# Attention and squared-ReLU MLP on one core: six small moves in a hand-scheduled order

## The chip, the cores and the metric

The kernel runs on one core of one Trainium2 chip. The metric is the time of one execution on the device, in microseconds (us), taken as the median of three runs. A core has a matrix engine (TensorE, PE in the profile), a vector engine (VectorE, DVE), an activation engine (ScalarE, ACT), a general engine (GpSimd, POOL) and a queue engine that issues DMA transfers (SyncE, SP). Each engine runs its own list of instructions in order, and waits for the others through semaphores.

## The reference

A transformer block for one sequence of 2048 positions and width 512, all in float32. `x` is normalized, projected to q, k and v, and each of 32 heads attends to eight positions, two apart, going back from its own; then comes `wo` and the residual. The result `h` is normalized again and goes through an MLP with 1792 hidden columns, whose activation is the square of the positive part.

```python
qkv = layernorm(x) @ wqkv                       # 2048x512 @ 512x1536, 32 heads of 16
idx = pos[:, None] - arange(8) * 2              # eight positions, masked where negative
attn = softmax(where(mask, q . k[idx] / 4, -1e9))
h = x + (attn . v[idx]) @ wo                    # 512x512
r = maximum(layernorm(h) @ w1 + b1, 0)          # 512x1792
out = h + (r * r) @ w2 + b2                     # 1792x512
```

## The kernel before, in words

Positions are handled in 16 tiles of 128. Every matrix product is made of three products: each operand is split into a high part in a short format (`xh`, `big_h`, `rh`, `th`; a cast on ACT, function `hi`) and a low part, the rest (`xl`, `big_l`, `rl`, `tl`; a subtraction on DVE or POOL, function `lo`). `mm3` issues the twelve matmuls of one such product: four slices of the contraction, three times.

The program has these stages. At the start, tile by tile, `x` is loaded, its statistics are taken (`x_stats`), it is normalized (`x_norm`), transposed on PE into a bank of accumulators (`x_T`) and split (`hi_T` casts on ACT, `lo_T` subtracts on DVE); q, k and v are made for the first four tiles in 16 slots (`n` in the code), and stored to memory in the order that attention needs. `first_phase(t0)` does q, k and v for the other tiles, two at a time, in slots of two halves (`m` counts halves). Attention is not done on PE: DVE multiplies q with k (`pr<-qp,k`) and the exponentials with v (`pr<-ex,v`), reduces (`ex<-pr`), and POOL adds up the products with v (`pr<-pr`, `o<-pr`). It runs beside the products all the time.

The second phase has passes `u` = 0, 1, 2 over four tiles of the hidden layer at a time: slot `p` does the product with one 128-column block of `w1` for the four tiles (`mm`, then `r`, `rh`, `rl`) and the product with `w2` of the block three slots earlier (`acc`). Between them the next four tiles are prepared: the attention output is transposed and split (`o_T`: `oh`, `ol`), multiplied with `wo` (`wo_product`), added to `x` (`h_add`, which takes the statistics too), normalized (`h_norm`), then b2 is added to it for the later residual (`add_b2`, on POOL), and it is stored (`spill`) until it is needed again (`unspill`). `h_T` transposes the normalized `h` and splits it into `big_l`. In the first pass `w2` is split too (`split_w2`: `w2_h`, and `w2_l` as a part of `big_l` or of `w_x`). The last stage handles the last four tiles in pairs of blocks with fewer products, from sums and differences of slices of `w1` (`t_load`, `t_sums`: `traw`; `t_split`: `th`, `tl`) and of `h` (`s`).

The order is set in the code by a small planner. Each slot has two lists of chores: `at(d, f)` puts `f` into the list run at the end of the slot `d` slots on, and `after(d, f)` into a second list, which is run after the attention of that slot was issued. Between the two, `pump` issues attention steps as long as the planned time of DVE (`now["dve"]`) is behind that of PE (`now["pe"]`). `dve(t)` adds `t` to DVE's planned time; a step of attention more or less in a slot follows from that. `HOLD` is 1.0. The tables `LH`, `OP`, `WP`, `HP`, `HL` give the slots in which `h` is loaded, `o_T`, `wo_product` and `h_T` come. `first_phase` has four banks for `mm` results, the second phase two (`Turn`).

Of the kernel before, what the change touches and what calls it, by code (L numbers as in the profile page):

```python
# [17 lines left out]
FB = F // P  # L18
# [12 lines left out]
SLOW = 1.01, 1.12, 1.08  # L31
DELAY = 3
WJ = 2
XT = 9, 11
OT = 4, 5, 10, 12
WO = 7, 9, 13, 15
HT = 20, 20, 21, 23
# [3 lines left out]
WP = 8, 9, 13, 14  # L41
# [5 lines left out]
HOLD = 1.0  # L47
# [5 lines left out]
def block_kernel(ctx, tc, x, wqkv, wo, w1, b1, w2, b2, out):  # L53
# [42 lines left out]
    def row(name, shape=(P, D), dt=F32):  # L96
        return work.tile(list(shape), dt, name=name, tag="row", bufs=ROWS)
# [4 lines left out]
    due = {}  # L102
    late = {}
    now = {"slot": 0, "pe": 0.0, "dve": 0.0, "sub": -1}

    def at(delta, fn, *a):
        due.setdefault(now["slot"] + delta, []).append((fn, a))

    def after(delta, fn, *a):
        late.setdefault(now["slot"] + delta, []).append((fn, a))  # L110
# [8 lines left out]
    def run(chores):  # L119
        todo = chores.get(now["slot"], [])  # L120
        while todo:
            fn, a = todo.pop(0)
            fn(*a)

    def dve(t):
        now["dve"] += t
# [10 lines left out]
    turn = {"mm": Turn("mm0", "mm1"), "tr": Turn("tr0", "tr1")}  # L137
# [58 lines left out]
    def transposes(src, banks="tr"):  # L196
        tr = turn[banks].tile("tr").rearrange("p (k c) -> p k c", k=KB)
        for k in range(KB):
            nc.tensor.transpose(tr[:, k, :], src[:, k * P:(k + 1) * P], ident)  # L199
        now["pe"] += 0.44  # L200
        return tr
# [14 lines left out]
    def mm3(ps, lh, ll, rh, rl, mid=None, at_=2 * KB):  # L216


        terms = [(lh, rh, k) for k in range(KB)] + [(ll, rh, k) for k in range(KB)]
        terms += [(lh, rl, k) for k in range(KB)]  # L220
        for n, (l, r, k) in enumerate(terms):
            if mid and n == at_:
                mid()
            nc.tensor.matmul(ps, l(k), r(k), start=(n == 0), stop=(n == 3 * KB - 1))  # L224
# [218 lines left out]
    def x_T(t):  # L443
        tr = transposes(xt.pop(t))
        xT[t] = row("xh", (P, KB, P), F32R), row("xl", (P, KB, P), F32R)
        at(0, hi_T, tr, [xT[t][0]])
        after(0, lo_T, tr, [xT[t][0]], [xT[t][1]])
# [62 lines left out]
    def qkv(t, gp, mid=None):  # L510

        ps = turn["mm"].tile("mm")
        xh, xl = xT[t]
        mm3(ps[:, :3 * GP], lambda k: xh[:, k, :], lambda k: xl[:, k, :],
            lambda k: pair(wq_h, k, gp), lambda k: pair(wq_l, k, gp), mid)
        at(1, evac, t, gp, None, ps)
# [79 lines left out]
    def wo_product(t, slots):  # L596
        ps = turn["mm"].tile("wo")
        oh, ol = oT.pop(t)
        mm3(ps, lambda k: oh[:, k, :], lambda k: ol[:, k, :],
            lambda k: wo_h[:, k, :], lambda k: wo_l[:, k, :])  # L600
        for n, (fn, a) in zip(slots, ((h_add, (t, ps)), (h_norm, (t,)), (add_b2, (t,)),
                                      (spill, (t,)))):
            (at if fn is h_add else after)(n, fn, *a)

# [3 lines left out]
    def h_T(t):  # L610
        if t // R == R - 1:
            return last_h_T(t)
        tr = transposes(hn.pop(t), "mm")
        i = t % R
        hs_, ls_ = [a[:, :, i] for a in hh], [a[:, :, i] for a in hl]
        due.setdefault(now["slot"], []).insert(0, (hi_T, (tr, hs_)))
        at(0, lo_T, tr, hs_, ls_)


# [266 lines left out]
    for n in range(16):  # L886
        gp, t = divmod(n, 4)
        qkv(t, gp, (lambda: start_T(t + 1)) if n < 3 else None)
        if n < 2:
            x_norm(n + 2)  # L890
        if n == 0:
            x_stats(3)
        if n < 6:
            for k in (0, 1):
                at(0, hi_wqkv, n // 2 + 1, n % 2 * 2 + k)
                after(0, lo_wqkv, n // 2 + 1, n % 2 * 2 + k,
                      nc.gpsimd if k or n < 2 else nc.vector)
        if n == 1:
            load_wqkv(3)
        if n == 13:  # L900
            consts()
        if n in (5, 6, 12, 14):
            at(0, load_x, n - 1 if n < 7 else n // 2)
        if n in (8, 9):
            at(0, x_stats, n - 4)
        if n in (12, 13):
            at(0, x_norm, n - 8)
        if n in (14, 15):
            x_T(n - 10)
        end_slot(2.09)  # L910


# [2 lines left out]
    def first_phase(t0):  # L915
        def chores(m):
            if t0 + 3 < 16:
                if m in (0, 2):
                    at(0, x_stats, t0 + 2 + m // 2)
                if m in (6, 7):  # L920
                    at(0, x_norm, t0 - 4 + m)
                if m in XT:
                    x_T(t0 + 2 + XT.index(m))
            if t0 + 5 < 16 and m in (6, 9):
                at(0, load_x, t0 + 2 + m // 3)
            if jobs and m % 3 == 0:
                at(0, weight_job)
            k = t0 // 2 * 12 - 72 + m
            if k == 19:
                dve(HOLD)  # L930
            for t in range(R):
                if k == OT[t]:
                    at(0, load_h, t)
                    o_T(t)
                if k == WO[t]:
                    wo_product(t, (1, 3, 4, 6))
                    now["pe"] += 2.73
                if k == HT[t]:
                    h_T(t)
            if k in W2:  # L940
                at(0, load_w2, W2.index(k))

        def half(m):
            end_slot(1.37)
            chores(m)

        for n in range(6):
            chores(2 * n)
            qkv_of(t0 + n % 2, n // 2, lambda: half(2 * n + 1))
            end_slot(1.37)  # L950
# [41 lines left out]
    for u in range(R - 1):  # L992
        now["sub"] = u
        first, end = u == 0, False
        fs = list(range(FB)) if first else [*sorted(place), 12, 13]
        fs += [f for f in range(12) if f not in fs and (u < 2 or f not in ENDS)]
        fs += ENDS if u == 2 else []
        need = [] if first else [f for f in fs if f < 12 and f not in place]
        acc = [psum.tile([P, D], F32, name="acc", tag=tag) for tag in ("acc0", "acc1", "tr0", "tr1")]
        js = range(R)  # L1000


        todo, halves = {}, {}
        for i in js:
            t = R * (u + 1) + i
            if not end:
                a = i // 2 if u == 2 else 0
                for p, *what in ((LH[i] - a, at, 0, load_h, t), (OP[i] - a, o_T, t),
                                 (WP[i] - a, wo_product, t, (0, 1, 2, 3))):
                    todo.setdefault(p, []).append(what)  # L1010
                p, h = (HP[i], i % 2) if u < 2 else HL[i]
                (todo, halves)[h].setdefault(p, []).append((h_T, t))
            todo.setdefault(UP[i], []).append((at, 0, unspill, R * u + i))
        if u == 2:
            for p, *what in ((12, at, 0, t_load, 0), (13, at, 0, t_load, 1), (13, after, 0, t_sums, 0),
                             (14, after, 0, t_sums, 1), (14, at, 1, t_split, 0),
                             (16, after, 1, t_split, 1)):
                todo.setdefault(p, []).append(what)

        def half(p):  # L1020
            run(due)
            for fn, *a in halves[p]:
                fn(*a)

        for p in range(FB + LAG):
            more = 0.0
            if p == FB:
                run(due)
                dve(HOLD)
            for fn, *a in sorted(todo.get(p, []), key=lambda x: x[0] is wo_product):  # L1030
                fn(*a)
                more += 2.73 if fn is wo_product else 0.0
            if p < FB:
                mlp1(u, fs[p])
                more += 2.73
                if first:
                    at(0, split_w2, p)
                    if p + 1 < FB:
                        load_w2(p + 1)
            q = p - LAG  # L1040
            if q >= 0:
                f = fs[q]
                mlp2(u, f, acc, js, q == 0, q == FB - 1,
                     (lambda: half(p)) if p in halves else None)
                more += 2.74
                if f < 12 and (need or first and p < FB - LAG):
                    free.append(place.pop(f))
                    if need:
                        at(1, fetch, need.pop(0))
            end_slot(more)  # L1050
        for i in js:
            at(u // 2, finish, R * u + i, acc[i])
# [3 lines left out]
    u = R - 1  # L1056
# [79 lines left out]
```

## Time and profile before

| what | value |
|---|---|
| median of 3 runs | 518.0 us (517.56 to 518.82) |
| the profiled execution, time | 518.24 us |
| its span, first to last instruction | 516.4 us |
| granted TensorE clock | 1.000 |
| PE busy | 509.3 us |
| DVE, POOL, ACT busy | 377.1, 348.9, 256.7 us |
| PE busy from 20 to 140 us | 119.43 of 120 us |
| PE busy from 214 to 260 us | 45.19 of 46 us |
| PE busy from 424 to 444 us | 19.80 of 20 us |
| memory traffic | 97.37 MB, mean 189 GB/s |

A row of the timeline gives the start and duration of an instruction in us, its engine, its line in the kernel, its operation, the tiles as output and inputs, their shapes, and how many like instructions follow each other; in brackets the idle time of the engine ahead of it and what released it. Busy times of PE are modelled at their ends, so its idle time is read better from the distance between starts.

### The profile page before, as it was taken

To read this page: it belongs to the slowest core of one execution; us is meant where nothing else is said; L and a number is where in the kernel's file an instruction comes from. 1 tells how busy PE (TensorE), PEld (TensorE's weight loads), DVE (VectorE), ACT (ScalarE), POOL (GpSimd) and SP (SyncE) were. 2 spreads that over 40 slices of the span, in tenths; PEclk is the share of its full clock that TensorE was granted. 3 is DMA by queue.
4 is the path that set the end of the run, shared out by engine and by line. 5 is a ranking of instruction groups with operands and counts; after the bars stand their busy time and mean duration, and the time that the engine had idled before them with its cause. 6 is when DMAs were issued, how large, how long until landed. Compare 5 with 4: busy or idle time off the path is not lost.

```text
span 516.4 us, 7610 instructions
## 1 busy us (share of the span) xinstructions
PE 509.3 (99%) x2508; PEld 430.4 (83%) x2508; DVE 377.1 (73%) x524; ACT 256.7 (50%) x498; POOL 348.9 (68%) x430
## 2 busy tenths in 40 slices
PE   8999999999999999999999999999999999999997
PEld 7998788888887888877888888888888888999996
DVE  5469899989997798978789799878883025842333
ACT  4624586767424753453364334246433425765542
POOL 4714789894785895796768759767799445585520
PEclk9999999999999999999999999999999999999999
DMA  8677889989767895666477627657541352444112
GB/s 267 182 211 202 247 292 314 285 262 285 236 190 191 276 313 176 176 190 210 137 252 227 174 91 223 202 169 249 177 135 39 102 161 81 159 131 141 64 41 82
DMA packets 88239, 97.37 MB, mean 189 GB/s; under 512 B 8328, under 2 KB 56712, under 8 KB 88200
## 3 DMA queue, kind: packets, MB, share of 16 engines
q1 hardware_dynamic: 87256, 96.37, 60.4%
q10 hardware_dynamic: 944, 0.52, 0.3%
q8 instruction: 19, 0.31, 0.2%
q14 instruction: 20, 0.16, 0.1%
HBM read 72.65 MB, written 24.25 MB: 188 GB/s over the span
## 4 chain that ended last, share of the span: by engine, by line
PE 51%; DVE 3%; DMA 2%; issue 1%; ACT 1%; POOL 1%; DVEq 0%; ACTq 0%
PE acc L805 23%; PE mm L224 15%; PE mm L728 6%; PE wo L224 5%; DMA k<-qkv_d 2%; PE tr L199 1%; DVE pr L335 1%; POOL big_l L144 0%; DVE big_l L144 0%; PE half L828 0%; POOL h L587 0%; ACT big_l L141 0%; DVE ex L369 0%; ACT wo_h L141 0%; DVE pr L346 0%
## 5 line engine op out<-in xcount | busy, mean ns | idle before, releaser
L403 POOL TENSOR_TENSOR pr<-pr 128x512 f32<-128x512 f32 (+1 forms) x128 | 131.9, 1031 | 52.2 <-DVE pr L346 47.0
L224 PE MATMUL mm<-big_l,w_h 128*128 128x512 f32 x336 | 89.6, 393 | 0.8 <-DVE ol L144 0.5
L335 DVE TENSOR_TENSOR pr<-qp,k 128x1024 f32<-128x1024 f32 x64 | 77.0, 1202 | 8.3 <-ACT qp L264 7.1
L346 DVE TENSOR_TENSOR pr<-ex,v 128x1024 f32<-128x1024 f32 x64 | 78.0, 1221 | 5.5 <-POOL o L403 2.9
L369 DVE TENSOR_REDUCE ex<-pr 128x64 f32<-128x1024 f32 x64 | 78.5, 1226 | 1.9
L224 PEld LDWEIGHTS mm<-big_l,w_h 128*128 128x128 f32 x336 | 62.3, 188 | 14.4 <-DVE ol L144 0.9
L144 POOL TENSOR_TENSOR rl<-r,rh 128x512 fp32r<-128x512 f32 x42 | 55.1, 1314 | 24.1 <-ACT rh L141 24.0
L781 ACT ACTIVATE r<-mm,b_sb 128x512 f32<-128x512 f32 x42 | 28.8, 686 | 58.4 <-PE mm L224 52.3
L224 PE MATMUL mm<-big_h,xl 128*128 128x512 f32 (+1 forms) x208 | 56.4, 380 | 0.6 <-DVE xl L144 0.3
L224 PE MATMUL mm<-big_h,xh 128*128 128x512 f32 (+1 forms) x208 | 53.3, 378 | 0.7 <-ACT xh L141 0.7
L805 PE MATMUL acc<-big_l,rh 128*128 128x512 f32 x190 | 52.7, 391 | 0.0
L224 PE MATMUL mm<-big_l,xh 128*128 128x512 f32 (+1 forms) x208 | 52.7, 375 | 0.0
L805 PE MATMUL acc<-big_h,rh 128*128 128x512 f32 x190 | 52.3, 392 | 0.0
L805 PE MATMUL acc<-big_h,rl 128*128 128x512 f32 x190 | 51.8, 390 | 0.0
L493 ACT COPY y<-mm 128x512 f32<-128x512 f32 (+1 forms) x52 | 28.6, 554 | 39.1 <-PE mm L224 26.3
L224 PE MATMUL mm<-big_l,w_l 128*128 128x512 f32 x168 | 45.0, 390 | 0.0
L224 PEld LDWEIGHTS mm<-big_h,xh 128*128 128x128 f32 x208 | 37.7, 188 | 7.2 <-ACT xh L141 1.8
L224 PEld LDWEIGHTS mm<-big_l,xh 128*128 128x128 f32 x208 | 38.2, 188 | 5.9
L224 PEld LDWEIGHTS mm<-big_h,xl 128*128 128x128 f32 x208 | 37.0, 188 | 6.7 <-DVE xl L144 1.9
L805 PEld LDWEIGHTS acc<-big_h,rl 128*128 128x128 f32 x190 | 35.7, 188 | 7.5
L805 PEld LDWEIGHTS acc<-big_l,rh 128*128 128x128 f32 x190 | 35.4, 188 | 7.2
L805 PEld LDWEIGHTS acc<-big_h,rh 128*128 128x128 f32 x190 | 34.8, 188 | 6.6
(148 smaller groups left out, 882.2 us busy)
## 6 DMA issues: line engine op xcount, KB each, us to landing
k<-qkv_d SPq DMA_DIRECT2D x48, 288.0 KB, 2.7
v<-qkv_d SPq DMA_DIRECT2D x48, 288.0 KB, 3.9
qkv_d<-y SPq DMA_DIRECT2D x18, 512.0 KB, 3.4
big_l<-w2l_d SPq DMA_DIRECT2D x24, 256.0 KB, 3.1
xt<-in_A_x_dram SPq DMA_DIRECT2D x16, 256.0 KB, 4.9
q<-qkv_d SPq DMA_DIRECT2D x32, 128.0 KB, 3.5
h<-in_A_x_dram SPq DMA_DIRECT2D x16, 256.0 KB, 3.5
h_d<-h SPq DMA_DIRECT2D x16, 256.0 KB, 3.7
```

What stands on the lines that cost most here:

```text
L144: eng.tensor_tensor(out=dst, in0=src, in1=h, op=ALU.subtract)
L199: nc.tensor.transpose(tr[:, k, :], src[:, k * P:(k + 1) * P], ident)
L224: nc.tensor.matmul(ps, l(k), r(k), start=(n == 0), stop=(n == 3 * KB - 1))
L335: nc.vector.tensor_tensor(out=pr.rearrange("p i w h d -> p i w (h d)"), in0=qps["now"][:, j % 2].unsqueeze(2).to_broadcast([P, RI, W, GC]) ...
L346: nc.vector.tensor_tensor(out=p2, in1=vwin, op=ALU.mult, in0=e1[:, :, :, j * GH:(j + 1) * GH].unsqueeze(4).to_broadcast([P, RI, W, GH, DH]))
L369: nc.vector.tensor_reduce(out=lf[:, :, :, j * GH:(j + 1) * GH], in_=pr, axis=X, op=ALU.add)
L403: nc.gpsimd.tensor_tensor(out=dst, in0=p2[:, :, :w], in1=p2[:, :, w:2 * w], op=ALU.add)
L493: nc.scalar.copy(y[:, :, t % RI * GC:(t % RI + 1) * GC], ps[:, :j * GC].rearrange("p (j c) -> p j c", j=j))
L728: nc.tensor.matmul(ps, sta[y][:, k], mov[x][:, k], start=(first and q == 0), stop=(last and q == len(terms) - 1), skip_group_check=True)
L781: nc.scalar.activation(r, ps, AF.Relu, bias=b1_sb[:, f:f + 1])
L805: nc.tensor.matmul(acc[j], l[:, j * P:(j + 1) * P], w[f], start=(first and n < len(js)), stop=(last and n >= len(terms) - len(js)))
```

## The change

Six places are touched.

1. `x_norm` and `x_T` of tiles 4 and 5 come one slot earlier at the start (`n` 11, 12 and 13, 14 instead of 12, 13 and 14, 15).
2. In `first_phase(12)`, `x_norm` of tiles 14 and 15 comes one half earlier, and their `x_T` at `m` = 7, 8 instead of 9, 11.
3. `h_T` puts the casts ahead of the other chores of the slot only if `mm` has two banks; with four banks they come in their turn.
4. `add_b2` goes into the first list of the next slot instead of the second list of its own. In pass 2, for the last two of the four tiles, `add_b2` and `spill` come three slots later still.
5. In passes 0 and 1 the planner's time of DVE is moved on by `HOLD` once more, at slot `p` = 12 (`FB - 2`).
6. In pass 2, the loads of the second pair, the sums and the splits of both pairs come a slot or two earlier.

```diff
-XT = 9, 11
+XT = (9, 11), (7, 8)
...
-            (at if fn is h_add else after)(n, fn, *a)
+            (after if fn in (h_norm, spill) else at)(n + (fn is add_b2), fn, *a)
...
-        due.setdefault(now["slot"], []).insert(0, (hi_T, (tr, hs_)))
+        if len(turn["mm"].tags) > 2:
+            at(0, hi_T, tr, hs_)
+        else:
+            due.setdefault(now["slot"], []).insert(0, (hi_T, (tr, hs_)))
         at(0, lo_T, tr, hs_, ls_)
...
-        if n in (12, 13):
-            at(0, x_norm, n - 8)
-        if n in (14, 15):
-            x_T(n - 10)
+        if n in (11, 12):
+            at(0, x_norm, n - 7)
+        if n in (13, 14):
+            x_T(n - 9)
...
-                if m in (6, 7):
-                    at(0, x_norm, t0 - 4 + m)
-                if m in XT:
-                    x_T(t0 + 2 + XT.index(m))
+
+                early = t0 == 12
+                if m + early in (6, 7):
+                    at(0, x_norm, t0 - 4 + m + early)
+                if m in XT[early]:
+                    x_T(t0 + 2 + XT[early].index(m))
...
-                                 (WP[i] - a, wo_product, t, (0, 1, 2, 3))):
+                                 (WP[i] - a, wo_product, t, (0, 1, 2 + 3 * a, 3 + 3 * a))):
...
-            for p, *what in ((12, at, 0, t_load, 0), (13, at, 0, t_load, 1), (13, after, 0, t_sums, 0),
-                             (14, after, 0, t_sums, 1), (14, at, 1, t_split, 0),
-                             (16, after, 1, t_split, 1)):
+            for p, *what in ((12, at, 0, t_load, 0), (12, at, 0, t_load, 1), (13, after, 0, t_sums, 0),
+                             (13, after, 0, t_sums, 1), (13, at, 1, t_split, 0),
+                             (14, after, 0, t_split, 1)):
...
+            if u < 2 and p == FB - 2:
                 dve(HOLD)
```

The rows that follow are the programs' instructions in issue order: line, operation, output and inputs, shape. First GpSimd in pass 0, around the low part of a block of `w2` (`big_l<-raw_2467`); `h<-h,b_sb` is `add_b2`, `o<-pr` the end of an attention sum. Before:

```order
L403 TENSOR_TENSOR o<-pr 128x2x64
L587 TENSOR_TENSOR h<-h,b_sb 128x512
L144 TENSOR_TENSOR big_l<-raw_2467,big_h 128x512
L144 TENSOR_TENSOR rl<-r,rh 128x512
L587 TENSOR_TENSOR h<-h,b_sb 128x512
L144 TENSOR_TENSOR rl<-r,rh 128x512
```

After:

```order
L403 TENSOR_TENSOR o<-pr 128x2x64
L144 TENSOR_TENSOR big_l<-raw_2467,big_h 128x512
L587 TENSOR_TENSOR h<-h,b_sb 128x512
L144 TENSOR_TENSOR rl<-r,rh 128x512
L587 TENSOR_TENSOR h<-h,b_sb 128x512
L144 TENSOR_TENSOR rl<-r,rh 128x512
```

The low part of `w2` now stands ahead of the addition of b2.

Next VectorE some ten microseconds later in the same pass: `w_x` is the low part of a block of `w2`, `ol` that of the attention output, `h<-wo,h` and the two rows behind it are `h_add`. Before:

```order
L346 TENSOR_TENSOR pr<-ex,v 128x1024
L369 TENSOR_REDUCE ex<-pr 128x16x4
L144 TENSOR_TENSOR w_x<-raw_2595,w_x 128x512
L144 TENSOR_TENSOR ol<-tr,oh 128x512
L577 TENSOR_TENSOR h<-wo,h 128x512
L152 BN_STATS st<-h 128x6
L153 BN_AGGR mv<-st 128x2
L335 TENSOR_TENSOR pr<-qp,k 128x1024
```

After:

```order
L346 TENSOR_TENSOR pr<-ex,v 128x1024
L144 TENSOR_TENSOR w_x<-raw_2594,w_x 128x512
L144 TENSOR_TENSOR ol<-tr,oh 128x512
L577 TENSOR_TENSOR h<-wo,h 128x512
L152 BN_STATS st<-h 128x6
L153 BN_AGGR mv<-st 128x2
L369 TENSOR_REDUCE ex<-pr 128x16x4
L335 TENSOR_TENSOR pr<-qp,k 128x1024
```

The reduction of attention moved behind `h_add`.

Last VectorE at the end of pass 2, from the last `h_add` to the split of `h` for the last stage; `traw` are the sums of the second pair, `big_l` and `s` parts of `h`. Before:

```order
L577 TENSOR_TENSOR h<-wo,h 128x512
L152 BN_STATS st<-h 128x6
L153 BN_AGGR mv<-st 128x2
L144 TENSOR_TENSOR big_l<-tr,big_l 128x2x128 x4
L696 TENSOR_TENSOR traw<-traw 128x2x128
L697 TENSOR_TENSOR traw<-traw 128x2x128
L698 TENSOR_TENSOR traw<-traw 128x2x128
L699 TENSOR_TENSOR traw<-traw 128x2x128
L663 TENSOR_TENSOR s<-tr,s 128x2x128
L664 TENSOR_TENSOR s<-s,tr 128x2x128
```

After:

```order
L577 TENSOR_TENSOR h<-wo,h 128x512
L152 BN_STATS st<-h 128x6
L153 BN_AGGR mv<-st 128x2
L699 TENSOR_TENSOR traw<-traw 128x2x128
L700 TENSOR_TENSOR traw<-traw 128x2x128
L701 TENSOR_TENSOR traw<-traw 128x2x128
L702 TENSOR_TENSOR traw<-traw 128x2x128
L144 TENSOR_TENSOR big_l<-tr,big_l 128x2x128 x4
L144 TENSOR_TENSOR tl<-traw,th 128x512
L666 TENSOR_TENSOR s<-tr,s 128x2x128
L667 TENSOR_TENSOR s<-s,tr 128x2x128
```

The four sums moved ahead of the splits of `h`, and a part of the second pair's split stands ahead of `s`.

More of the change, by code (lines that the diff above doesn't have):

```diff
@@ L1028, in block_kernel @@
                 run(due)
+                dve(HOLD)
+            if u < 2 and p == FB - 2:
                 dve(HOLD)
```

## The prediction

> **What bounds the kernel now.** I read the engine table first, then TensorE's waits, then the chain that ended last, and then TensorE's timeline row by row, because the table alone shows only that TensorE (PE) is never long idle.
>
> ```profile
> PE 509.3 (99%) x2508; PEld 430.4 (83%) x2508; DVE 377.1 (73%) x524; ACT 256.7 (50%) x498; POOL 348.9 (68%) x430
> ...
> PE mm L224 <- DVE ol L144: 0.5, 1, 0.5
> PE tr L199 <- ACT y L493: 0.4, 1, 0.4
> PE mm L224 <- ACT r L781: 0.3, 1, 0.3
> ...
> 241.27 2.72 PE acc L805 x12
> ```
>
> The reader is to see that the whole span is one stream of matmuls, and that the waits are single events of half a microsecond. The last line is a piece of the chain: 12 matmuls of 512 columns take 2.72 us, 0.227 each, so 4 in a row take 0.91. Wherever the next group starts later than that, PE stood still. Only such stops can be won, since the change leaves the number of matmuls alone. In all rows below the first number is the start, the second the duration, and the bracket the idle time and its releaser.
>
> **The start, x's fifth and sixth parts.** The change puts their normalization and transposes one slot ahead.
>
> ```profile
> 44.82 1.17 PE L224 MATMUL mm<-big_h,xh 128*128 128x512 f32 x4
> 46.31 1.21 PE L224 MATMUL mm<-big_h,xl 128*128 128x512 f32 x4 [0.32 <-DVE xl L144]
> ...
> 48.28 1.08 PE L224 MATMUL mm<-big_h,xh 128*128 128x512 f32 x4
> 49.49 1.19 PE L224 MATMUL mm<-big_h,xl 128*128 128x512 f32 x4
> ...
> 58.28 0.29 DVE L358 TENSOR_REDUCE sm<-ex 128x16 f32<-128x128 f32 x1 [1.56 <-ACT ex L392]
> 63.75 0.68 DVE L144 TENSOR_TENSOR xl<-tr,xh 128x512 fp32r<-128x512 f32 x1
> ...
> 64.49 1.19 PE L224 MATMUL mm<-big_h,xl 128*128 128x512 f32 x4
> ```
>
> The two stops are 1.49 - 0.91 = 0.58 and 1.21 - 0.91 = 0.30, together 0.88. In the new order both xl stand ahead of attention work on VectorE (DVE), so they go. But the seventh part's xl keeps its place, and the matmul at 64.49 starts right when it ends (63.75 + 0.68 = 64.43). That xl is not set by PE: DVE had waited 1.56 at 58.28 for an exponential of ScalarE (ACT) and worked without a pause from there. If PE comes 0.88 sooner, it waits 0.88 longer at 64.49. I count 0; the bounds are 0.88 won (if the exponential comes sooner too) and a loss of the 0.30 that one such stop cost. The move of parts 14 and 15 near 140 us has no PE stop beside it; it stands at 0, between the same bounds of one stop, 0.30 either way.
>
> **The copy ahead of h's parts.**
>
> ```profile
> 157.56 1.20 ACT L141 CAST big_l<-tr 128x256 fp32r<-128x256 f32 x4 [2.30 <-PE tr L199]
> 158.62 0.63 ACT L493 COPY y<-mm 128x512 f32<-128x512 f32 x1
> ...
> 158.28 0.61 PE L224 MATMUL mm<-big_h,xl 128*128 128x512 f32 x2
> 159.30 0.65 PE L199 MATMUL tr<-ident,hn 128*128 128x128 f32 x4 [0.41 <-ACT y L493]
> ```
>
> The third transposes need the bank that y empties, and y stands behind four casts of 1.20 us. PE lost 1.02 - 2 x 0.227 = 0.57. With y ahead of the casts it is done about 1.1 sooner. The casts then end 0.6 later (y's length); the products that read them belong to the next phase, and each lo part on DVE waits for its own cast only. Gain 0.57; bounds 0 and 0.57, the loss excluded since nothing else waits for these casts.
>
> **b2's addition a slot later.**
>
> ```profile
> 225.01 1.29 POOL L587 TENSOR_TENSOR h<-h,b_sb 128x512 f32<-128x512 f32 x1
> 226.26 1.81 POOL L144 TENSOR_TENSOR big_l<-raw,big_h 128x512 fp32r<-128x512 f32 x1
> ...
> 228.11 0.69 ACT L781 ACTIVATE r<-mm,b_sb 128x512 f32<-128x512 f32 x1 [3.67 <-POOL big_l L144]
> ...
> 227.90 0.60 PE L199 MATMUL tr<-ident,o 128*128 128x128 f32 x4
> 228.85 1.19 PE L224 MATMUL mm<-big_l,w_h 128*128 128x512 f32 x4 [0.35 <-ACT r L781]
> ...
> 252.94 0.60 PE L199 MATMUL tr<-ident,hn 128*128 128x128 f32 x4
> 253.29 1.63 PE L805 MATMUL acc<-w_x,rh 128*128 128x512 f32 x6
> ```
>
> PE waits for r, r for big_l, and big_l stood behind the 1.29 of the addition on GpSimd (POOL). Four transposes hold PE 0.35 (252.94 to 253.29), so this stop is 0.95 - 0.35 = 0.60. The new order has big_l first, and r is ready 1.25 sooner: the stop goes. The addition ends where big_l ended, about 228.1; the store of h, queued on SyncE (SP) behind other transfers, was not issued before that anyway.
>
> **Less attention in two slots.** The first two passes of the second phase hold one attention step (1.0 us of the planner's clock) two slots ahead of the end.
>
> ```profile
> 235.72 1.23 DVE L369 TENSOR_REDUCE ex<-pr 128x64 f32<-128x1024 f32 x1
> 236.85 0.75 DVE L144 TENSOR_TENSOR w_x<-raw,w_x 128x512 fp32r<-128x512 f32 x1
> 237.53 0.68 DVE L144 TENSOR_TENSOR ol<-tr,oh 128x512 fp32r<-128x512 f32 x1
> ...
> 236.72 1.07 PE L224 MATMUL wo<-wo_l,ohl 128*128 128x512 f32 x4
> 238.26 1.19 PE L224 MATMUL mm<-big_l,w_h 128*128 128x512 f32 x4 [0.47 <-DVE ol L144]
> ...
> 235.88 0.62 ACT L141 CAST w_x<-raw 128x512 fp32r<-128x512 f32 x1 [0.22 <-DMA raw<-in_B_w_dram]
> ...
> 228.10 0.32 SPq L984 DMA_DIRECT2D w2l_d<-big_l  x1
> ...
> 230.45 0.38 SPq L954 DMA_DIRECT2D raw<-in_B_w_dram  x1
> ```
>
> The stop is 238.26 - 236.72 - 0.91 = 0.63. The reduction (1.23) moves behind ol and h's addition, so w_x can start at 235.72 instead of 236.85, and ol ends at 238.21 - 1.13 = 237.08. Counting the 0.60 of the stop before, PE asks for ol at 237.03. So the two stops together (1.23) bring what ol allows, 1.13 or a little more. This has a condition: w_x's cast waited for its load until 235.88, the load was issued at 230.45, and SP had stood at 228.10 until POOL's big_l was done. Since big_l now ends some 1.25 sooner, the load does too, and the cast at about 234.9 is in time. Were it not, w_x could start only at 236.50 and ol would end at 237.9: the two stops would bring 0.3. I take 1.13, bounds 0.3 and 1.23.
>
> In the other pass the same hold lets DVE write h's last lo parts ahead of a reduction:
>
> ```profile
> 346.52 1.09 PE L805 MATMUL acc<-big_h,rl 128*128 128x512 f32 x4
> 347.63 1.17 PE L224 MATMUL mm<-big_l,w_h 128*128 128x512 f32 x4
> ...
> 250.85 0.76 DVE L144 TENSOR_TENSOR big_l<-tr,big_l 128x256 fp32r<-128x256 f32 x2 [0.56 <-ACT big_l L141]
> ```
>
> That stop is 1.11 - 0.91 = 0.20 and goes (bounds 0 and 0.20). What was held has to be done later: in the first pass a product with v (1.22 by the row of the same length, 1.23 for a reduction) now stands behind the fourth addition to h, and delays the softmax subtraction, ACT's exponential, the norm behind it and the casts. The lo parts of 250.85 would end at 251.61 + 1.22 = 252.83, and the transposes that need their bank start at 252.94. That leaves 0.11. I count 0; if the chain is later still, the loss is what exceeds 0.11.
>
> **The first pairs' weight sums a slot sooner.**
>
> ```profile
> 433.74 1.39 DVE L699 TENSOR_TENSOR traw<-traw 128x256 f32<-128x256 f32 x1
> ...
> 436.25 1.29 POOL L587 TENSOR_TENSOR h<-h,b_sb 128x512 f32<-128x512 f32 x1
> ...
> 436.46 1.35 DVE L144 TENSOR_TENSOR big_l<-s,big_l 128x256 fp32r<-128x256 f32 x1
> 439.08 0.43 DVE L144 TENSOR_TENSOR big_l<-s,big_l 128x256 fp32r<-128x256 f32 x1
> ...
> 438.59 0.40 PE L728 MATMUL mm<-big_l,w_h 128*128 128x256 f32 x2
> 443.02 0.50 PE L728 MATMUL mm<-wo_h,th 128*128 128x256 f32 x2
> ```
>
> From 438.59 to 443.02 PE issues 30 matmuls of 256 columns; at half of 0.227 they need 3.4, and PE took 4.43. Some 0.1 of that is the slower rate of short matmuls, so the three stops are about 0.9. They come from h's last splits on DVE, which stood behind the four sums (the last of 1.39), and one of which took 1.35 beside POOL's addition at 436.25 against 0.43 alone. Now the sums fall into DVE's idle time after the last addition to h, and POOL's addition goes into the last stage. The split chain ends 1.15 + 0.92 sooner: all 0.9 goes (bounds 0 and 0.9). The second pair's four loads move a slot ahead on SP too, and the last two stores of h a slot back, where they hold up a load of w2 by the time that POOL's addition takes; these loads are issued several slots before their use, so I count 0. POOL's two additions (2 x 1.29) now stand around the third pair's sums, and the tl behind them has, by an estimate, half a microsecond of room.
>
> That DVE and POOL can block each other is what 436.46 shows. The Trainium skill (SBUF — State Buffer, "Who interferes with whom") says it more strictly: a VectorE instruction with two SBUF inputs and a GpSimd instruction that reads SBUF exclude each other for the whole instruction. This row agrees; no row of before shows the moved additions in their new place.
>
> **The sum.** 0.57 + 1.13 + 0.20 + 0.9 = 2.8; the first multiplications after each stop are slower as well (46.31 to the next group), which I do not price, and set against the tight places. 2.8 to 3.0, say 2.9. The profiled execution took 518.24, 0.24 above the median of the runs; it would become 515.3, and the median 515.1. I predict 515.2.
>
> **The rivals.**
> - The early stops are kept too. If the exponential at 58 us follows PE, the 0.88 is won: 514.3. Against it speaks DVE's unbroken work from 58.28.
> - A new gate gives 1 to 2 us back. Either w_x's load does not move (0.8 lost: 516.0), or a moved POOL addition meets a two-input DVE instruction that PE waits for, 1.35 - 0.43 = 0.92 each, two of them 1.84: 517.0. For it: it is what 436.46 did. Against it: POOL's additions now stand where DVE has short work. By the page's rule every such meeting costs its length; the rows leave it open.
> - The change does nothing on balance: stops are replaced by the part that was next late, 517.5 to 518.5. For it speaks the narrow room (0.11 and 0.05) at two places; against it that five places are independent.
> - Slower: the held attention is late at the end of its pass. A whole step (product, reduction, product with v: about 3.65) then stands before h's last norms; beyond the 0.11 of room PE waits 3.5 in a pass. That decides if DVE's queue has no idle time left there: 518.8 for one pass, 522.3 for both. Against it: DVE idles 0.56 at 250.85 alone, and only one instruction of 1.2 is held, not a step.
>
> **How the numbers follow.** Forecast (514.4 to 516.2) 0.55; early stops kept 0.10; a new gate (516.2 to 517.3) 0.18; nothing on balance 0.09; slower 0.08. A measurement of this kernel can tell 0.3% (1.55 us) from no change, so faster means under 516.45: the first two and a quarter of the third, 0.69. Slower means over 519.55: 0.05, the second half of the last case. The rest is 0.26. The range from 513.9 to 517.6 leaves out half of the second case, most of the fourth and the last; the forecast's own is 514.4 to 516.2.
>
> **What would show it.** After the change the waits of PE should no longer name ol, y and r; at 64 us the wait for xl should have grown to about 1.2; POOL's big_l should come ahead of h near 225; the three stops after 438 should be gone. Wrong would be a new wait of PE near 250 (casts or lo parts), one for tl in the last stage, or a wait for r or ol that stays.

## The result, and the profile after

The changed kernel takes 515.25 us (median of 9 runs, 514.67 to 517.83) against 517.99 us (9 runs, 517.50 to 518.96): 2.74 us less, a ratio of 0.9950 with a 95% interval of 0.9937 to 0.9962. The profiled execution took 514.81 us, 3.43 less than the profiled one of before; its span is 513.0 us. So the two profiles differ by 0.7 us more than the medians do. That remainder is one of the things to explain.

The engine table, and the waits of TensorE (PE), of the changed kernel:

```profile
PE 506.4 (99%) x2508; PEld 429.3 (84%) x2508; DVE 376.7 (73%) x524; ACT 256.2 (50%) x498; POOL 350.0 (68%) x430
```

```profile
PE tr L856 <- POOL mhalf L842: 1.3, 1, 1.3
PE tr L199 <- DVE xt L190: 1.1, 1, 1.1
PE mm L224 <- ACT xh L141: 0.7, 1, 0.7
PE mm L224 <- DVE xl L144: 0.2, 1, 0.2
```

The busy times hardly move. What went is in the waits: ol, y and r are gone from the list; xl stays once, the rest is the first ten microseconds. Where the time was won is read best from the start of the same matmul in both traces; the difference runs ahead at each stop that went, and falls back at each new one. All starts are from the traces of before and after:

| matmul of before, start | start after | ahead by | what lies in between |
|---|---|---|---|
| 64.49 mm<-big_h,xl | 63.45 | 1.03 | the two stops at 46 and 49 us, with the slower matmuls behind them |
| 160.95 mm<-big_l,xh | 159.38 | 1.57 | the stop for y (0.55) |
| 228.85 mm<-big_l,w_h | 226.70 | 2.14 | the stop for r (0.57, and 0.04 behind it) |
| 249.94 acc<-w_x,rh | 247.11 | 2.84 | the stop for ol (0.66) |
| 299.95 acc<-w_x,rh | 297.35 | 2.60 | a new stop near 252 us (-0.24) |
| 438.59 mm<-big_l,w_h | 435.71 | 2.88 | the stop at 347.63 (0.28) |
| 447.67 acc<-big_h,rh | 443.86 | 3.81 | three stops of the last splits (0.93) |
| 460.00 mm<-wo_l,w_h | 456.58 | 3.42 | a new stop near 450 us (-0.39) |
| 513.05, the last | 509.64 | 3.42 | nothing |

In the table a stop counts with the slower matmuls right behind it, up to 0.1. The rows of PE's timeline after at the places that the prediction speaks of:

```profile
157.78 0.60 PE L199 MATMUL tr<-ident,hn 128*128 128x128 f32 x4
...
226.35 0.60 PE L199 MATMUL tr<-ident,o 128*128 128x128 f32 x4
226.70 1.17 PE L224 MATMUL mm<-big_l,w_h 128*128 128x512 f32 x4
...
234.56 1.08 PE L224 MATMUL wo<-wo_l,ohl 128*128 128x512 f32 x4
235.47 1.13 PE L224 MATMUL mm<-big_l,w_h 128*128 128x512 f32 x4
...
438.58 0.40 PE L731 MATMUL mm<-big_l,w_h 128*128 128x256 f32 x2
438.82 0.40 PE L731 MATMUL mm<-big_l,w_l 128*128 128x256 f32 x2
439.06 0.40 PE L731 MATMUL mm<-big_l,w_h 128*128 128x256 f32 x2
439.31 0.40 PE L731 MATMUL mm<-wo_h,th 128*128 128x256 f32 x2
```

From the transposes at 226.35 to the product it is 0.35, the bare length of four transposes; from 234.56 to 235.47 it is 0.91, four matmuls. Pairs of short matmuls near 439 us follow each other every 0.24 without a gap: all three stops after 438 us are gone. The reasons on VectorE (DVE) and ScalarE (ACT):

```profile
234.06 0.68 DVE L144 TENSOR_TENSOR w_x<-raw,w_x 128x512 fp32r<-128x512 f32 x1
234.66 0.68 DVE L144 TENSOR_TENSOR ol<-tr,oh 128x512 fp32r<-128x512 f32 x1
235.67 0.69 DVE L577 TENSOR_TENSOR h<-wo,h 128x512 f32<-128x512 f32 x1 [0.33 <-PE wo L224]
...
155.78 0.59 ACT L493 COPY y<-mm 128x512 f32<-128x512 f32 x1 [1.43 <-PE mm L224]
156.26 1.21 ACT L141 CAST big_l<-tr 128x256 fp32r<-128x256 f32 x4
...
224.78 0.69 ACT L784 ACTIVATE r<-mm,b_sb 128x512 f32<-128x512 f32 x1 [1.89 <-POOL big_l L144]
```

ol ends at 235.34, 0.13 ahead of the product at 235.47, where before it was 0.6 behind; that product does not read ol, it waits for the bank of accumulators that ol empties. y comes ahead of the casts. r ends at 225.47, 1.2 ahead of PE.

The two new stops, on PE and on what releases it (GpSimd is POOL):

```profile
252.10 0.65 PE L199 MATMUL tr<-ident,hn 128*128 128x128 f32 x4
...
251.23 0.82 ACT L194 ACTIVATE hn<-h,rs 128x512 f32<-128x512 f32 x1 [1.57 <-POOL rs L162]
...
247.19 2.13 POOL L403 TENSOR_TENSOR pr<-pr 128x512 f32<-128x512 f32 x2
249.40 0.47 POOL L403 TENSOR_TENSOR o<-pr 128x128 f32<-128x128 f32 x1
249.95 0.23 POOL L158 TENSOR_SCALAR rs<-mv 128x1 f32<-128x1 f32 x1
...
446.27 1.76 POOL L587 TENSOR_TENSOR h<-h,b_sb 128x512 f32<-128x512 f32 x1
447.98 1.76 POOL L144 TENSOR_TENSOR tl<-traw,th 128x512 fp32r<-128x512 f32 x1
...
449.25 0.40 PE L731 MATMUL mm<-big_l,th 128*128 128x256 f32 x2
449.79 0.50 PE L731 MATMUL mm<-big_l,tl 128*128 128x256 f32 x2
```

Near 252 us the last norm of h waits for three small instructions (rs; the first is shown) on POOL, and these stand behind an attention sum, as they did before. POOL had worked without a pause since 240.76, where another sum had waited 3.50 for DVE's product with v; the hold has put a reduction (1.20) between the addition to h and that product. The norm ends at 252.05, and the transposes start at 252.10. Near 450 us tl ends at 449.74, behind an addition of b2 that took 1.76; PE goes on at 449.79.

### The profile page after: what moved, and what is told of

Same layout as the page of the kernel before. It is cut to its first block, busy times and chain, and to the rows that moved or that the text cites. A ratio compares the mean times of both kernels' runs of the same rounds, so it can differ in the third digit from the quotient of the medians.

```text
span 513.0 us, 7625 instructions
## 1 busy us (share of the span) xinstructions
PE 506.4 (99%) x2508; PEld 429.3 (84%) x2508; DVE 376.7 (73%) x524; ACT 256.2 (50%) x498; POOL 350.0 (68%) x430
## 4 chain that ended last, share of the span: by engine, by line
PE 92%; POOL 3%; DMA 2%; DVE 1%; issue 1%; ACT 1%; SPq 0%; POOLq 0%; ACTq 0%
PE mm L224 45%; PE acc L808 29%; PE wo L224 9%; PE mm L731 6%; PE tr L199 4%; DMA wraw<-in_A_wqkv_dram 1%; DMA qkv_d<-y 1%; POOL pr L403 1%; POOL h L587 1%; POOL tl L144 0%; PE half L831 0%; SPq L432 0%; POOL wo_l L144 0%; DVE pr L346 0%; DVE ex L369 0%
## 5 line engine op out<-in xcount | busy, mean ns | idle before, releaser
L346 DVE TENSOR_TENSOR pr<-ex,v 128x1024 f32<-128x1024 f32 x64 | 78.0, 1221 | 11.6 <-POOL o L403 7.6
L493 ACT COPY y<-mm 128x512 f32<-128x512 f32 (+1 forms) x52 | 28.6, 552 | 40.0 <-PE mm L224 30.1
```

The lines of the kernel that those rows point to most:

```text
L346: nc.vector.tensor_tensor(out=p2, in1=vwin, op=ALU.mult, in0=e1[:, :, :, j * GH:(j + 1) * GH].unsqueeze(4).to_broadcast([P, RI, W, GH, DH]))
L493: nc.scalar.copy(y[:, :, t % RI * GC:(t % RI + 1) * GC], ps[:, :j * GC].rearrange("p (j c) -> p j c", j=j))
```

## The experiments

Each kernel was timed against the kernel before on the same chip. Times below are medians; the stops are from each run's own trace. The changed kernel's 515.25 us, to which differences are taken, comes from its own comparison. The intervals of the ratios reach 0.0012 to 0.0026 either way, 0.6 to 1.3 us, so a difference of medians under about 1 us is not told from nothing by itself; where a smaller one is read below, it is read from the traces.

**The start: two kernels that change only that part.** The first is the kernel before with the first hunk of the change, the second the changed kernel without it.

```diff
-        if n in (12, 13):
-            at(0, x_norm, n - 8)
-        if n in (14, 15):
-            x_T(n - 10)
+        if n in (11, 12):
+            at(0, x_norm, n - 7)
+        if n in (13, 14):
+            x_T(n - 9)
```

> The kernel before with only the start's part of the change (x_norm and x_T of tiles 4 and 5 a slot earlier). Theory 1: the stop near 64 us follows PE, so the 0.9 us of the two early stops is kept: 0.9 faster than before, stop near 64 us still about 0.3 us. Theory 2: the xl of the seventh part is paced by a store of q, k and v that lands near 33 us, and what is won at 46 and 49 us is waited for at 64 us: 0 to 0.3 us faster in the median, and in the trace the end of that xl follows the landing of the store by 30 to 31 us (before 64.43 - 33.88 = 30.55, after 63.40 - 32.25 = 31.15), with a stop near 64 us that is longer where the store lands late.

> The changed kernel without the start's part. Theory 1: two stops near 46 and 49 us are back and it is 0.9 us slower than the changed kernel (about 516.1). Theory 2: the stops are back, but the stop near 64 us shrinks by as much, and it is 0 to 0.3 us slower (about 515.4).

The first took 517.75 against 517.87 of before, a ratio of 0.9998 (0.9985 to 1.0011): no difference that these runs can tell. The second took 515.67 (ratio to before 0.9966, 0.9940 to 0.9992), 0.4 above the changed kernel's median, which these runs can't tell from nothing. What is plain is in its trace. It has the old order, and yet no stop near 46 and 49 us, which neither theory expected. Its stop near 64 us is there in full. What differs between the executions is when transfers land. The row to compare is ACT's copy of y near 33 us, which waits for the store of an older y to land. First before (with two more of its rows, for below), then after, then these two, each with the xl near 64 us:

```profile
32.05 0.69 DVE L152 BATCH_NORM_STATS2 st<-xt 128x6 f32<-128x512 f32 x1 [3.17 <-DMA xt<-in_A_x_dram]
...
33.98 0.86 ACT L493 COPY y<-mm 128x384 f32<-128x384 f32 x2 [5.86 <-DMA qkv_d<-y]
...
56.78 0.59 ACT L493 COPY y<-mm 128x512 f32<-128x512 f32 x1 [0.69 <-DMA qkv_d<-y]
```

```profile
32.35 0.86 ACT L493 COPY y<-mm 128x384 f32<-128x384 f32 x2 [4.36 <-DMA qkv_d<-y]
...
62.72 0.68 DVE L144 TENSOR_TENSOR xl<-tr,xh 128x512 fp32r<-128x512 f32 x1
```

```profile
32.80 0.86 ACT L493 COPY y<-mm 128x384 f32<-128x384 f32 x2 [5.09 <-DMA qkv_d<-y]
...
62.37 0.68 DVE L144 TENSOR_TENSOR xl<-tr,xh 128x512 fp32r<-128x512 f32 x1
63.10 1.19 PE L224 MATMUL mm<-big_h,xl 128*128 128x512 f32 x4 [0.20 <-DVE xl L144]
```

```profile
32.61 0.86 ACT L493 COPY y<-mm 128x384 f32<-128x384 f32 x2 [4.65 <-DMA qkv_d<-y]
...
62.83 0.68 DVE L144 TENSOR_TENSOR xl<-tr,xh 128x512 fp32r<-128x512 f32 x1
63.57 1.20 PE L224 MATMUL mm<-big_h,xl 128*128 128x512 f32 x4 [0.17 <-DVE xl L144]
```

The profile of before came from an execution in which this store landed late, at 33.88. In the others with the loads in the old place it landed between 32.2 and 33.3, and the xl near 64 us ended 29.6 to 31.2 us behind the landing. The landing varies by 1.7 us among executions, and the start's part of the change alone did not move the median: so the first row of the table above is, as far as these runs can tell, luck of the two profiled executions. It is enough for the 0.7 us by which the profiles differ more than the medians. No trace has the new order with a landing as late as that of before.

The early landing is one link of a chain and not the gate itself: between 32.2 and 33.3 it does not order the executions (the xl ends at 62.60 with the landing at 33.02, at 63.33 with 32.21). The copy of y near 55 us is nearer to the gate: in all thirteen traces the xl ends 7.65 or 7.66 us behind its start (before 56.78 and 64.43), and in eleven of them the profile names the landing of a later store as what it waited for, in two a product of PE. The exponential that VectorE (DVE) waits for stands behind this copy on ACT, so by the names in eleven traces it follows transfers and not PE.

**The transfers that pace the start.** If that is so, the stores should be made to land sooner. Two loads of x, 0.5 MB, stand ahead of the early one in the queue of SyncE (SP); here they are issued behind it, and the statistics that need them come a slot later on DVE. Once this is done in the kernel before, alone, and once together with two repairs that are told below.

```diff
-        if n in (5, 6, 12, 14):
-            at(0, load_x, n - 1 if n < 7 else n // 2)
-        if n in (8, 9):
-            at(0, x_stats, n - 4)
+        if n == 7:
+            at(0, load_x, 4)
+            at(0, load_x, 5)
+        if n in (12, 14):
+            at(0, load_x, n // 2)
+        if n in (9, 10):
+            at(0, x_stats, n - 5)
```

> The kernel before, with only the loads of x's tiles 4 and 5 issued behind the first pair of stores that attention waits for. Theory 1: the landing of that store paces the attention of the start, so that all three xl stops of before (near 46, 49 and 64 us) go or shrink: 0.6 to 1.3 us faster than before, about 517. Theory 2: in the kernel before, the stops near 46 and 49 us come from the order on VectorE alone: only the one near 64 us can go, 0 to 0.4 us faster.

> The kernel with both repairs, and at the start the loads of x's tiles 4 and 5 issued behind the first pair of stores of q, k and v that attention waits for, instead of ahead of it. Theory 1: the landing of that store (32.2 to 33.9 us in the runs so far) sets the xl near 64 us; without 0.5 MB ahead of it in the queue it lands 1 to 2 us sooner, the xl comes sooner by as much, and the stop of 0.45 near 64 us goes: 0.4 us faster than with the repairs alone, about 514.2. Theory 2: the xl is set by later transfers, and nothing changes at 64 us; or the statistics of tiles 4 and 5 come late on VectorE and cost up to 1 us near 40 us.

Alone it took 516.68 against 517.52 of before, a ratio of 0.9983 (0.9970 to 0.9995), 0.84 us less. No xl stop is left in its trace, which is of an execution of 518.43, 1.75 above the median, with PE behind by more than a microsecond since the first 12 us. Together with the repairs it took 513.58 (513.55 to 515.24), a ratio of 0.9931 (0.9909 to 0.9952): 1.0 below the repairs alone, more than expected; in the traces the two are 0.89 apart from 64 us on, about half of it the stop there. Its rows:

```profile
31.45 0.48 ACT L493 COPY y<-mm 128x384 f32<-128x384 f32 x1 [3.58 <-PE mm L224]
...
60.88 0.68 DVE L144 TENSOR_TENSOR xl<-tr,xh 128x512 fp32r<-128x512 f32 x1
...
61.99 1.09 PE L224 MATMUL mm<-big_h,xh 128*128 128x512 f32 x4
62.92 1.07 PE L224 MATMUL mm<-big_h,xl 128*128 128x512 f32 x4
```

This copy now waits for PE and no longer for the landing, the xl is 1.4 us ahead of its reader, and the matmuls near 62 us follow without a gap. The start is paced by transfers, then, and the start's part of the change is worth nothing that these runs can tell; that is theory 2 of the first pair, except that the stop near 64 us does not grow with a later landing. By which way the loads' new place helps is not separated: DVE no longer waits for x's load ahead of attention either (3.17 at 32.05 in the trace of before), since the statistics moved too.

**The hold and b2's addition.** First the changed kernel without the hold, then with b2's addition back in its own slot.

```diff
-            if u < 2 and p == FB - 2:
-                dve(HOLD)
```

> The changed kernel without the hold at slot 12 of passes 0 and 1. Theory 1: the stops for r and for ol hang together, since ol's time is set by VectorE and GpSimd and not by PE: a stop of about 1.2 us for ol comes back near 237 us, the stop of 0.27 near 345 us too, and the new stop of 0.23 near 252 us goes: 1.2 us slower than the changed kernel. Theory 2: the two gains add up independently: a stop of 0.63, and 0.67 us slower. Theory 3: ol was late only because the load for w_x came late, which the move of b2's addition cures: no stop for ol, and no difference.

```diff
-            (after if fn in (h_norm, spill) else at)(n + (fn is add_b2), fn, *a)
+            (at if fn is h_add else after)(n, fn, *a)
```

> The changed kernel with all additions of b2 back at the end of their own slot (the last two of pass 2 still three slots late). Theory 1 (the sum as predicted): the stop for r near 226 us comes back with 0.6; ol then has 0.6 more time, but the load of w_x waits behind big_l again, so ol keeps a stop of up to 0.25; the addition ahead of the last stage's first product leaves tl in time and takes the 0.4 away there: 0.2 to 0.5 us slower than the changed kernel. Theory 2: the hold alone sets ol, and POOL's order does not matter: no stop for r, 0.4 faster.

Without the hold: 516.20, a ratio of 0.9972 (0.9958 to 0.9986), 0.95 above the changed kernel. The rows of this kernel:

```profile
233.94 1.23 DVE L369 TENSOR_REDUCE ex<-pr 128x64 f32<-128x1024 f32 x1
235.07 0.74 DVE L144 TENSOR_TENSOR w_x<-raw,w_x 128x512 fp32r<-128x512 f32 x1
235.74 0.68 DVE L144 TENSOR_TENSOR ol<-tr,oh 128x512 fp32r<-128x512 f32 x1
...
234.40 1.08 PE L224 MATMUL wo<-wo_l,ohl 128*128 128x512 f32 x4
236.47 0.74 PE L224 MATMUL mm<-big_l,w_h 128*128 128x512 f32 x2 [1.00 <-DVE ol L144]
```

The stop for ol is 236.47 - 234.40 - 0.91 = 1.16, not the 0.63 of before: what PE won at r it waits for at ol, as theory 1 said. The stop of 0.2 near 345 us is back too, and that near 252 us is gone, with rs 0.5 earlier and PE 1.1 later there.

With the addition back: 515.16 (ratio 0.9945, 0.9927 to 0.9962), no slower than the changed kernel. Its trace, again PE's rows:

```profile
225.86 0.60 PE L199 MATMUL tr<-ident,o 128*128 128x128 f32 x4
226.81 1.21 PE L224 MATMUL mm<-big_l,w_h 128*128 128x512 f32 x4 [0.36 <-ACT r L784]
...
234.72 1.08 PE L224 MATMUL wo<-wo_l,ohl 128*128 128x512 f32 x4
235.85 0.98 PE L224 MATMUL mm<-big_l,w_h 128*128 128x512 f32 x3
```

The stop for r is back with 0.6, and ol keeps a stop of 0.22. That fits theory 1: w_x's cast on ACT waits 0.17 for its load and ends 0.45 later than in the changed kernel. But the subtraction of w_x (233.57, 1.61 instead of 0.68) also meets POOL's rl (233.35 to 234.65), and either could hold it that long, so the load is not shown to be the cause. In return the stop near 450 us is gone, since one addition comes earlier there; the one near 252 us is gone because PE comes 0.5 later; and in this execution the stop near 64 us is gone as well. So the move of b2's addition is worth 0.8 us at r and ol, and what it wins is taken back in part near 252 and 450 us, by 0.2 and 0.4.

**The copy, and tiles 14 and 15.** The changed kernel with the casts ahead of y again, and with tiles 14 and 15 in their old places.

```diff
-        if len(turn["mm"].tags) > 2:
-            at(0, hi_T, tr, hs_)
-        else:
-            due.setdefault(now["slot"], []).insert(0, (hi_T, (tr, hs_)))
+        due.setdefault(now["slot"], []).insert(0, (hi_T, (tr, hs_)))
```

> The changed kernel with the casts of h's parts ahead of the copy of y again in the first phase. Theory 1: PE stops 0.57 us near 158 us for y, and nothing later takes it up: 0.57 us slower than the changed kernel (about 515.8). Theory 2: a later gate that PE reaches too early anyway (ol near 236, tl near 450) takes it up: 0 to 0.2 us slower.

```diff
-                early = t0 == 12
+                early = False
```

> The changed kernel with tiles 14 and 15 of x normalized and transposed where they were before (part 2 undone). Theory 1: no PE stop stands beside them in either order, so no difference (within 0.2 us of the changed kernel, no new stop between 120 and 160 us). Theory 2: the earlier transposes made room on VectorE ahead of h's statistics: a stop of 0.3 us or more between 135 and 160 us comes, and it is as much slower.

The first took 515.75 (ratio 0.9959, 0.9944 to 0.9974), 0.50 above the changed kernel; its waits have "PE tr L199 <- ACT y L493: 0.4, 1, 0.4" again, and the trace the stop of 0.56 at 158.57. That is theory 1 by the trace, where nothing later takes the stop up; the medians alone do not tell it from theory 2. The second took 515.14 (ratio 0.9952, 0.9938 to 0.9967), 0.1 below the changed kernel, and no stop between 120 and 160 us in its trace: no difference.

**The last stage.** The changed kernel with the last two additions in their old slots, so that POOL does them in its idle time ahead of the last stage; then with the loads, sums and splits of the first pairs in theirs.

```diff
-                                 (WP[i] - a, wo_product, t, (0, 1, 2 + 3 * a, 3 + 3 * a))):
+                                 (WP[i] - a, wo_product, t, (0, 1, 2, 3))):
```

> The changed kernel with the last two additions of b2 in pass 2 in their old slots (plus the one slot that all additions moved), so that GpSimd does both before the last stage's first product instead of around the third pair's sums. Theory 1: the new stop of 0.40 us for tl near 450 us comes from the addition ahead of tl: it goes, and the split of h has enough room for what the additions cost beside it: 0.4 us faster than the changed kernel. Theory 2: each addition blocks a two-input VectorE instruction of the split for 0.9 us, as at 436.46 before: the stops after 438 us come back with up to 0.9, and it is up to 0.5 us slower.

```diff
-            for p, *what in ((12, at, 0, t_load, 0), (12, at, 0, t_load, 1), (13, after, 0, t_sums, 0),
-                             (13, after, 0, t_sums, 1), (13, at, 1, t_split, 0),
-                             (14, after, 0, t_split, 1)):
+            for p, *what in ((12, at, 0, t_load, 0), (13, at, 0, t_load, 1), (13, after, 0, t_sums, 0),
+                             (14, after, 0, t_sums, 1), (14, at, 1, t_split, 0),
+                             (16, after, 1, t_split, 1)):
```

> The changed kernel with loads, sums and splits of the first two pairs back in their old slots; the last two additions of b2 stay in the last stage. Theory 1: the split of h was late by two things, the four sums ahead of it (1.15) and the addition beside it (0.92), and PE's stops were about 0.95; taking away either is nearly enough, as the run with the additions back showed for the sums: stops after 435 us of 0 to 0.2, at most 0.2 us slower than the changed kernel. Theory 2: the sums are the cause: stops of 0.5 to 0.9 come back, and it is 0.5 to 0.9 slower.

With the additions back it took 515.03 (ratio 0.9949, 0.9930 to 0.9967). No stop after 430 us is left in its trace, though the addition does what it did before:

```profile
432.82 2.73 POOL L587 TENSOR_TENSOR h<-h,b_sb 128x512 f32<-128x512 f32 x2
...
433.05 1.35 DVE L144 TENSOR_TENSOR big_l<-s,big_l 128x256 fp32r<-128x256 f32 x1
...
435.66 0.42 DVE L144 TENSOR_TENSOR big_l<-s,big_l 128x256 fp32r<-128x256 f32 x1
```

The split beside the first addition takes 1.35 again, the one at 435.66 takes 0.42: one delay of 0.93, which the earlier sums have made room for. The median is 0.2 below the changed kernel. In this execution the matmul near 64 us started at 64.02, 0.57 later than in the trace of after, and the last matmul of all ended only 0.17 later: the 0.4 that theory 1 expected.

With the pairs back it took 516.13 (ratio 0.9972, 0.9958 to 0.9986), 0.88 above the changed kernel. Here neither theory was right. The three stops of before shrink to one of 0.23 at 439.62, which is theory 1; but the second pair's split is late as well (its tl on POOL runs from 440.38 to 442.19, and the third pair's sums behind it end 1.6 later than in the changed kernel), and that makes stops (slower matmuls included) of 0.23 at 442.24, 0.40 at 449.45 and 0.55 at 450.96, where the changed kernel has 0.39. The loss is as large as theory 2 said, for another reason.

**Both repairs.** The additions as above, and the three small instructions for tile 7's norm ahead of the attention sum.

```diff
-            after(0, finish)
+            (at if key == 7 else after)(0, finish)
```

> The changed kernel with two repairs: the last two additions of b2 in pass 2 in GpSimd's idle time before the last stage's first product, and, for h's tile 7, GpSimd's three small statistics instructions ahead of an attention sum instead of behind it. Theory 1: both new stops of the change go (0.40 for tl near 450 us, 0.23 for the norm near 252 us), 0.6 faster than the changed kernel, about 514.6. Theory 2: the attention sum that moves 1.1 us back is late for the next transposes of the attention output, and a wait of up to 1 us takes the place of the 0.23.

It took 514.57 (514.42 to 514.99), a ratio of 0.9942 (0.9922 to 0.9961), 0.7 below the changed kernel. Of its waits, one stands behind the first ten microseconds:

```profile
PE mm L224 <- DVE xl L144: 0.2, 1, 0.2
```

It is the stop near 64 us, the only one left. With x's loads behind the store that goes too; 513.58 us is the fastest version, 4.5 us below the kernel before.

## Why the prediction was right, and where it was not

Forecast were 515.2 us and a gain; 515.25 was measured. That the number was met so closely is partly luck: the gains came out larger than worked out, and two new stops that the sum had at 0 took 0.63. The mechanism, single stops of PE that an order can take away, is what the table and the runs show. Its terms one by one:

- The copy, 0.57: the table shows 0.55, undoing it costs a stop of 0.56. Right.
- The addition of b2 and the hold together, 1.13: the table shows 1.27. The reasoning that ol is the common gate is what the run without the hold shows (1.16). The condition on w_x's load fits the run with the addition back (a stop of 0.22 with the hold in place), but is not shown apart from POOL's rl beside it. The size was 0.14 low: DVE finished ol about 0.2 earlier than worked out, so that the whole stop went, and 0.04 are slower matmuls.
- The lo parts near 347 us, 0.20: 0.28 with the slower matmuls behind the stop, which the sum left out.
- The pairs, 0.9: 0.93 in the table. The reason given, that the split chain ends 1.15 + 0.92 sooner, left room for either one alone; the run with the additions back shows it for the first.
- "Half a microsecond of room" for the tl behind POOL's additions: this step failed. It was an estimate without rows. With the additions elsewhere (both repairs) tl ends at 448.31, 1.2 ahead of its reader; here it ended at 449.74, and the stop cost 0.39. The second addition took 1.76 beside a subtraction on DVE; with 1.29, by an estimate from these rows, tl would have ended 0.2 ahead of its reader. In the runs without the start's part and with tiles 14 and 15 back it took 1.29 and the stop is there all the same, because the sum ahead of it took 1.27 instead of 0.74. In each, POOL lost half a microsecond beside DVE, for which the estimate had no term.
- The tail of the first pass, 0.11 of room: the casts and lo parts named there were in time. What was late was rs on POOL, which the working did not follow: 0.24 lost. Putting rs ahead of the sum (both repairs) took the stop away. The prediction named a wait near 250 us as what would make it wrong, but by another chain.
- The start, 0: right in the medians (0.9998 for that part alone), wrong in what the profile was to show. The wait near 64 us did not grow to 1.2; it was 0.41 before and 0.45 after, with the slower matmuls behind it. The prediction argued that the exponential does not follow PE, which holds by eleven of the thirteen traces, but it took the stops at 46 and 49 us for a fixed property of the kernel. They were those of one execution whose transfers landed late.

Without its first row the table adds up to 2.39. The four gains brought 3.03 where 2.8 was worked out, and the two new stops took 0.63 where nothing was; the 2.9 of the forecast was 0.5 too much for what the order itself does in these two traces. The median moved by 2.74, with an interval of 2.0 to 3.3 (0.9962 and 0.9937 of 518) that holds both numbers, so what lies between 2.39 and 2.74 is not settled.

The rival of a new gate was half true: a moved addition did come in the way of something that PE waits for, with 0.39 instead of 0.92. The slower rival showed in small: the held attention made h's last norm late, through POOL, for 0.24 in one pass instead of 3.5.

On POOL and DVE at once: 433.05 beside 432.82 is the same event as before, and there the rule of the Trainium skill (SBUF — State Buffer, "Who interferes with whom") agrees: the DVE instruction with two inputs ends (434.40) after the first of the two additions does (434.11). The rule speaks of two inputs in SBUF, the on-chip memory of the tiles. The product with v is no such case, since the kernel keeps ex in a bank of accumulators (`logits` in the code) and only v in SBUF; it keeps its mean of 1221 ns over 64 of them while POOL is busy 68% of the span, and the 22 that ran almost wholly beside POOL are no longer than the others.

```profile
L346 DVE TENSOR_TENSOR pr<-ex,v 128x1024 f32<-128x1024 f32 x64 | 78.0, 1221 | 11.6 <-POOL o L403 7.6
```

## What to carry to other kernels

When one engine is busy 99%, list every place where its next instruction starts later than its own cadence, and ask for each which engine sets it and what comes late next; gains at two places on one chain are worth what the common gate allows. A stop that hangs on a transfer's landing is not a property of the order alone: look at it in several executions before an order is changed for it, and try to move what stands ahead of that transfer. Moving work out of the way of one engine moves it in front of something else; small instructions that a norm or a split waits for should stand ahead of long ones that nothing waits for.

## What was not expected of the hardware

The same pair of stores, issued within 0.9 us of the same time in eleven executions, landed between 32.2 and 33.9 us. Only the latest one had the two stops at 46 and 49 us, together 0.9 us; the other with the old order and an early landing had none. Additions on POOL that take 1.29 alone took 1.76 and 1.83 beside DVE subtractions (446.27, and 224.70 in the trace of after), so a delay falls on either side.
